# Query and key weights issued from ScalarE's DMA queue, token blocks left on SyncE's, and 14 more filler matmuls

## The chip, the cores and the metric

The kernel runs on one core of one Trainium2 chip. The metric is the device time of one execution in microseconds. Thirteen executions of the kernel before are at hand, and one more look at it with the hardware profiler on, which is itself one of the executions timed.

## The reference

A transformer block on 2048 tokens of 640 features, in bfloat16. With everything that is only shape taken out:

```python
h  = x + attn(layernorm(x), wq, wk, wv, wo, beta)     # x: [1, 2048, 640]
h2 = h + silu(layernorm(h) @ w1) @ w2                 # w1: [640, 1728]
# attn: 32 heads of 20, 4 segments of 512 tokens, one after the other
q, k, v = x @ wq, x @ wk, x @ wv                      # each weight [640, 640]
for s in range(4):
    p     = softmax(q_s @ k_s.T * 20**-0.5 + causal_mask)
    a_mem = (phi(q_s) @ M) / (phi(q_s) @ z + 1e-6)    # phi(t) = t+1 if t>0 else exp(t)
    o_s   = g * a_mem + (1 - g) * (p @ v_s)           # g = sigmoid(beta)
    M, z  = M + phi(k_s).T @ v_s, z + sum(phi(k_s))
out = concat(o) @ wo
```

## The kernel before

**Tiling.** Tokens come in blocks of 128, four blocks to a segment. Each of the four segments goes through the same stages: layer norm of its blocks (`n1_st`, `n1_rs`, `n1_ap` for statistics, reciprocal root and application), transposition into `xT`, projections `pr` to queries and keys (line 801) and `v` to values (line 773), scores `qk` (line 874), their exponentials `e` on ScalarE (line 885), causal masks on GpSimd (line 897), products with the values `av` (line 920), normalisation into `otok`, the output projection `wo` (line 1102), a second layer norm, and the two layers of the feed-forward part, `h1` (line 1126) and `h2` (line 1157). Stages of neighbouring segments are interleaved.

**Order.** Nothing is scheduled at run time. The table `ORDER` (line 355) lists every task by name, with the buffer slots that it takes and, behind a slash, the engine where there is a choice (`/A` ScalarE, `/D` VectorE). Each task, when its turn in the table comes, appends its instructions to the list of its engine; so the order on one engine is the order of the table cut down to that engine's tasks. `Tracker.add` (line 79) works out which semaphores each instruction has to wait for, and `Tracker.emit` (line 160) writes the lists, a wait in front of the instruction that needs it. Every transfer has a semaphore of its own.

**Transfers.** All go through the helper `dma` (line 535), which puts them on SyncE's list (`SP` in the code; `AC` is ScalarE). `load_x` (line 559) fetches token blocks, `load_w` (line 564) weights. The first nine transfers have no wait ahead of them: four token blocks (`x0`, `x2`, `x1`, `x3`, 160 KB each, in this order), then `w_q` (800 KB), `beta` (128 copies of 64 bytes), `w_k` (800 KB), `w_wv` (800 KB) and the next four blocks in one transfer (`x4`, 640 KB).

**The first 20 us.** TensorE begins with `fill54`: 54 matmuls of 256 columns on a tile of zeros (line 607), whose result nobody reads. Then come the transposes `n1_tp0` to `n1_tp3` (line 731), which read the normalised blocks. Their results are moved from PSUM to `xT` by `n1_te0`, `n1_te1` and `n1_te3` on ScalarE and `n1_te2` on VectorE (lines 740, 741). The raw query and key weights land in a part of the buffer `sT` and are rearranged head by head into `wqr` and `wkr` by `re_wq0` to `re_wq4` and `re_wk0` to `re_wk4`, some on VectorE (line 688), some on ScalarE (line 686). The first projections are `pr000` and `pr010`, which need the first two parts of `wqr`, then `pr001` and `pr011`, which need those of `wkr`; their results go to `QK` by `qe` tasks (lines 811, 812). GpSimd sets up constants and pads of the value tile meanwhile (`vpad1`, lines 614 to 616).

The place of the weights in the table, before the change, is this (first lines of `ORDER`; `w_q` and `w_k` are tasks of SyncE, so their place counts only against SyncE's other tasks):

```python
zpad:0 iota sel epsc x0:0 vpad0 mt2 x2:1 n1_st0:0 x1:2 x3:3 w_q:0 n1_st2:2 mta2 halfc mt0 mt1 n1_rs0 n1_st1:1
n1_st3:3 epsg0 n1_ap0:0 n1_rs2 fill54:0 n1_tp0:0 n1_te0/A:0 n1_rs1 n1_rs3 n1_ap1:1 n1_ap2:2 n1_tp1:2 n1_te1/A
n1_ap3:0 re_wq0/D:0 n1_tp2:4 n1_te2/D n1_tp3:6 n1_te3/A beta pr000:4 w_k zf0 re_wq1/A pr010:6 lsc0 re_wk0/D:0
```

A filler `fillN:S` writes N times into PSUM slot S; it waits until what was in that slot has been read. There are two besides `fill54`: `fill2` and `fill4`, near 160 us.

Of the kernel before, what the change touches and what calls it, by code (L numbers as in the profile page):

```python
# [324 lines left out]
D = 640  # L325
# [32 lines left out]
n1_ap3:0 re_wq0/D:0 n1_tp2:4 n1_te2/D n1_tp3:6 n1_te3/A beta pr000:4 w_k zf0 re_wq1/A pr010:6 lsc0 re_wk0/D:0  # L358
re_wk2/A pr001:5 re_wk1/D lsc1 mta1 lsc2 re_wk3/A qe000/D:0 pr011:7 w_wv:0 x4:4,5,6,7 qe001/A qe011/A:0 ex011:0 lsc3
re_wq4/D re_wq2/D pr020:5 qk0x0:0 e0x2:0 e0x0 qe010/D pr031:7 pr021:6 qk1x0:0 vpad1 mtb1 mm5 mm1 mk0x n1_st5:3  # L360
qe020/D:0 ph011:0 qe021/D n1_rs5 v00:4 n1_st6:1 n1_ap5:0 re_wk4/D qe031/A:0 re_wq3/A ex001:1 n1_st4:3 n1_st7:2
e1x2:1 e1x0 v01:6 mk1x pr030:0 ve00/A:0 ex021:0 ve01/A qk2x0:4 qe030/A av1x:1 ex031:2 av0x:2 e2x2:0 pr041:3 pr040:0
oe1x/A:0 e2x0 mt3 n1_rs4 qk3x0:4 e3x0:1 e3x2 n1_rs7 mta3 mtb3 mm11 mk2x n1_rs6 vt06:0 oe0x/D:1 ph001:1 vt09 kt01:0
vt03 tn0x:1 qe041/D:0 kt00:1 ex041:1 v03:2 qe040/D ph031:0 qk0yb0:4 nm0x:0,0 v02:0 e0yb2:0 ve03/D ph021:1 e0yb0
qk0ya0:4 tn1x:2 ve02/D nm1x:0 e0ya2:0 e0ya0 mk0yb mk3x av2x:3 oe2x/D:0 qk4x0:0 av0y:4 e4x2:0 e4x0 n1_ap6:2 av3x:6
mz00:5 tn2x:7 oe0y/D:1 oe3x/D:0 zf1 n1_ap7:1 nm2x:0 qk1yb0:0 vt00 vt010 vt08 vt01 ma00/A:0 e1yb2:0 e1yb0 n1_ap4:3
vt05 n1_tr5:0 mk4x v11:4 ve11/A:1 mk1yb mtb2 mm10 vt07 n1_tr6 vt04 vt011 vt02 mz01:7 qk1ya0:0 tn0y:6 nm0y:0 ma01/D:1
v12:4 ve12/D av4x:7 e1ya2:0 e1ya0 n1_tr4 n1_tr7 oe4x/A:1 tn3x:6 qk5x0:0 e5x0:0 e5x2 mm3 mk5x tn4x:7 nm3x:0 v10:4
qk6x0:0 kt03:0 nm4x:1 e6x0:1 kt02:1 v13:6 e6x2 ve10/D av5x:4 oe5x/D:1 ve13/A qk7x0:0 pr100:5 qe100/D:0 ph041:1
e7x0:0 mz02:4 e7x2 ma02/A:2 mk6x av6x:6 qk2yb0:0 mta0 mk7x e2yb2:1 e2yb0 mk2yb mtb0 tn5x:5 pr101:4 w_w2_1:0 w_w1_0:0  # L370
w_wo:0 oe6x/D:1 av7x:6 nm5x:1 av1y:7 w_w1_3 oe7x/D:0 qk2ya0:0 ex100:1 tn6x:6 qe101/D e2ya2:0 e2ya0 nm6x:1 ex101:0
pr130:5 tn7x:6 pr110:4 nm7x:1 qk3ya0:0 pr111:6 qe110/A:0 ph100:0 ph101:0 pr121:4 oe1y/D:0 ot0:0 qe111/D e3ya2:1
e3ya0 qk3yb0:0 e3yb0:0 wo0:6 qe130/D:0 e3yb2 qe121/D:0 ex110:0 rs0 w_w1_1 ot1 mm0 mzc0 av2y:4 oe2y/A:1 n2_st0:3
qk4ya0:0 mm9 mzc1 mk3yb mm6 mzc6 n2_rs0 mm2 wo1:6 rs1 n2_st1:1 w_w2_0 w_w1_4 n2_ap0:1 e4ya2:0 e4ya0 mz03:4 w_w1_2
qk4yb0:0 kt10:1 e4yb2:1 e4yb0 av3y:5 tn2y:6 pr141:7 n2_rs1 n2_tr0:0 mzc2 mzc3 mb00:0 mk4yb ma03/D:3 nm2y:1 n2_ap1:3
n2_tr1 ex111:1 qk5ya0:0 pr140:4 oe3y/A:1 qe141/A:0 tn3y:7 e5ya0:1 nm3y:1 e5ya2 pr120:6 mz10:7 tn1y:5 qk5yb0:0
qe120/A qe140/D av4y:4 ma10 nm1y:1 oe4y/D:0 ph110:0 e5yb2:0 h1_0_8_0:5 e5yb0 h1_0_1_0:7 th0_8_0:0 ex140:2 th0_1_0:1
tn4y:4 qk6ya0:0 pr131:6 e6ya2:0 e6ya0 s0_1_0:0 nm4y:1 s0_8_0 ph111:0 h1_0_0_0:7 th0_0_0:0 w_w2_2 s0_0_0 qe131/D
mk5yb h1_0_13_0:4 th0_13_0:1 qk6yb0:0 h1_0_10_0:5 h1_0_11_0:7 av5y:6 s0_13_0 e6yb0:1 e6yb2 w_w2_4 x8:8,9,10,11
kt11:1 w_w2_3 qk7ya0:0 h1_0_9_0:4 th0_10_0:1 th0_11_0:0 s0_10_0 e7ya0:1 s0_11_0 h1_0_7_0:5 th0_9_0:0 th0_7_0:1  # L380
oe5y/D:0 epsg1 e7ya2 tn5y:6 nm5y:1 s0_9_0 h1_0_2_0:7 h1_0_5_0:6 th0_2_0:0 s0_7_0 mk6yb mm4 th0_5_0:1 qk7yb0:0
e7yb2:0 ph140:0 s0_5_0 s0_2_0 h1_0_3_0:5 th0_3_0:1 h1_0_6_0:4 h1_0_4_0:6 av6y:7 e7yb0 s0_3_0 th0_4_0:1 s0_4_0
qk8a0:0 n1_st11:1 h1_0_12_0:5 th0_6_0:0 oe6y/A:0 s0_6_0 e8a0:0 mk7yb e8a2 h2_0_0:6 n1_st10:3 n1_rs10 mk8a av7y:4
th0_12_0:0 qk8b0:0 e8b0:0 ex120:2 e8b2 ex141:1 s0_12_0 n1_st8:2 n1_rs8 oe7y/D:1 n1_st9:0 n1_rs9 h2_0_1 h2_0_2 h2_0_3
qk8e0:0 e8e0:0 e8e2 ex130:0 n1_ap8:3 o0 h2_1_0:4 ph141:0 tn6y:6 tn7y:7 h2_1_1 vt16:0 mk8e ex131:1 mk8b qk9a0:0
e9a0:1 e9a2 nm7y:1 h2_1_2 h2_1_3 kt04:0 vt12 mz04:7 qk9b0:0 nm6y:0 n1_tr8:0 vt10 ph131:1 vt13 ot2 o1 mzc10 n1_ap9:3
mzc4 n1_rs11 av8:6 wo2:4 n1_ap11:1 ma04/A:4 ph120:0 rs2 e9b2:1 e9b0 oe8/A:1 qk10a0:0 vt18 tn8:6 ot3 out0 n1_tr9 vt19
nm8:0,0 n1_ap10:3 n1_tr11 e10a0:0 e10a2 wo3:4 qk10b0:0 n1_tr10 vt14 ex121:2 mk9b mb01:0 mk9a ad8:0 av9:6 e10b0:0
e10b2 rs3 oe9/D:1 kt14:0 vt110 n2_st3:3 mk10a mm7 qk10e0:4 e10e2:0 e10e0 mzc7 n2_rs3 mk10b mz11:0 ma11 tn9:2 pr200:1
nm9:0,0 n2_st2:1 n2_ap3:3 qk11a0:4 e11a0:1 e11a2 pr201:0 v20:2 mk10e mk11a mzc5 qk11b0:4 n2_rs2 mb02:0 mm8 mzc8  # L390
qe201/A:0 e11b0:1 ve20/D:0 e11b2 pr211:0 qe200/D av10:2 qk12a0:4 oe10/A:1 vt15 mzc9 mzc11 mb04:0 mk11b vt11 mb03:0
n2_ap2:1 qe211/D:0 e12a2:0 e12a0 ad9 tn10:2 nm10:0,1 ph130:0 kt13:1 out1 vt111 n2_tr2 n2_tr3 v21:0 ve21/A qk12b0:4
av11:2 vt17 oe11/D:1 ph121:1 mz14:0 e12b0:0 e12b2 ma14 h1_0_1_1:1 th0_1_1:0 h1_0_4_1:2 th0_4_1:1 qk13a0:4 e13a2:1
e13a0 kt12:0 h1_0_2_1:3 s0_1_1 s0_4_1 tn11:0 pr231:2 qk12e0:4 th0_2_1:1 nm11:0,0 mk13a mk12b mz13:0 mk12a s0_2_1
e12e2:0 e12e0 h1_0_6_1:3 qe231/D:0 h1_0_5_1:2 mz12:1 ma13 qk13b0:4 th0_5_1:1 th0_6_1:0 s0_5_1 s0_6_1 ma12 h1_0_8_1:0
mk12e h1_0_9_1:2 e13b0:1 e13b2 av12:1 qk14a0:4 pr210:3 th0_8_1:0 oe12/D:1 s0_8_1 v23:0 e14a2:0 th0_9_1:0 e14a0
qk14b0:4 e14b0:0 e14b2 s0_9_1 qe210/D ve23/D h1_0_7_1:3 h1_0_3_1:2 pr221:0 qk14e0:4 qe221/D:0 th0_3_1:0 th0_7_1:1
mk13b s0_3_1 mk14a e14e0:1 e14e2 s0_7_1 mk14b h1_0_10_1:1 av13:0 h1_0_0_1:3 qk15a0:4 ad11 mk14e ad10 oe13/D:0
th0_10_1:1 th0_0_1:0 s0_0_1 s0_10_1 pr241:0 tn12:2 av14:1 e15a2:1 e15a0 qk15b0:4 qe241/D:0 pr220:0 oe14/A:1
h1_0_13_1:1 e15b2:0 e15b0 nm12:0,1 mk15a th0_13_1:1 qe220/D mk15b ad12 s0_13_1 tn14:2 nm14:0,0 ex201:2 v22:4 ve22/A  # L400
ex220:0 tn13:0 av15:2 nm13:0,1 qk16a0:4 pr230:3 oe15/A:0 tn15:0 ph201:1 qe230/D e16a2:1 vt29:0 ad13 mb10:0 mb12:0
ad14 nm15:0,1 e16a0 h1_0_12_1:2 ex231:2 ad15 h1_0_11_1:3 th0_12_1:1 ex211:1 qk16b0:4 e16b0:0 e16b2 mk16b h2_2_0:0
h2_2_1 s0_12_1 th0_11_1:1 mk16a ph211:0 qk16e0:4 e16e2:1 s0_11_1 pr240:2 h2_2_2 ex200:1 ph200:0 h2_2_3 o2 e16e0
qe240/A ph220:0 ot5:0 qk17b0:4 wo5:2 ot6 ot4 vt26 e17b2:1 e17b0 rs5 mk16e mb13:0 av16:0 ph231:2 ex241:0 n2_st5:1
oe16/A:0 qk17a0:4 e17a2:1 wo4:2 e17a0 kt23:0 out2 ot7 rs4 n2_st4:3 ex210:2 kt20:1 vt211 ph210:0 h2_3_0:0 qk18b0:4
tn16:2 h2_3_1 h2_3_2 nm16:0,1 e18b0:0 e18b2 qk18e0:4 mk17b mb14:0 h2_3_3 n2_rs4 n2_rs5 wo7:2 n2_ap4:3 n2_tr4:0 mk18b
mk17a ex230:2 e18e2:0 e18e0 o3 qk18a0:4 n2_ap5:1 rs7 n2_st7:1 out3 mk18e ad16:0 vt22 vt20 e18a0:0 wo6:0 x12 vt21
n2_tr5 e18a2 av17:2 qk19b0:4 mk18a rs6 n2_st6:3 n2_rs7 e19b2:1 e19b0 oe17/A:0 mb11:0 n2_rs6 mz20:3 av18:0 mz23:1
ma20 n2_ap7:3 fill2:3 qk19a0:4 oe18/D:1 n2_tr7 e19a0:0 e19a2 mk19b mk19a n2_ap6:2 ma23 n2_tr6 vt210 vt24 tn18:2
nm18:0,1 vt25 vt28 vt27 vt23 fill4:0 tn17:0 qk20a0:4 e20a0:1 av19:2 e20a2 oe19/A:0 n1_st13:3 h1_1_0_0:3 th1_0_0:1  # L410
n1_st15:1 qk20b0:4 e20b0:1 nm17:0,0 ph241:1 s1_0_0:0 n1_st12:0 h1_1_1_0:2 e20b2 h1_1_3_0:0 th1_1_0:1 h1_1_7_0:3
th1_3_0:0 ex240:0 qk21b0:4 h1_1_2_0:1 e21b2:0 e21b0 ad18 n1_rs15 s1_1_0 n1_rs13 n1_rs12 n1_ap12:2 n1_ap15:3 mk20b
s1_3_0 n1_st14:1 th1_7_0:0 s1_7_0 h1_1_5_0:2 n1_rs14 th1_5_0:1 qk20e0:4 e20e2:0 h1_1_9_0:0 s1_5_0 n1_tr15:0 n1_tr12
n1_ap14:1 h1_1_10_0:3 th1_2_0:0 h1_1_4_0:2 th1_9_0:1 ex221:1 e20e0 s1_2_0 n1_tr14 s1_9_0 th1_10_0:1 s1_10_0 mk20a
mk21b mk20e th1_4_0:0 v30:0 qk21a0:4 n1_ap13:1 ve30/D:1 s1_4_0 ph230:0 e21a2:0 h1_1_6_0:3 v32:0 e21a0 qk22a0:4
av20:2 n1_tr13 kt21:0 mk21a ad17 th1_6_0:0 s1_6_0 av21:3 ve32/A tn19:0 oe20/D:1 nm19:0,0 pr311:2 e22a2:1 e22a0
# [33 lines left out]
def build(nc, es, A_x, A_wq, A_wk, A_wv, A_wo, A_beta, B_x, B_w1, B_w2, out):  # L450
    T = Tracker()
# [77 lines left out]
    def R(*items):  # L529
        r = []  # L530
        for a, subs in items:
            r += a.keys(subs)
        return r

    def dma(name, reads, writes, fn, prio, bw, kind="plain", lane=None, after=None):
        ln = T.lane(name) if lane is None else lane

        def emit(eng):
# [691 lines left out]
```

## Time and profile before

| | us |
|---|---|
| median of 13 executions | 320.0 (318.1 to 322.41) |
| the profiled execution | 321.41 |
| its span, first to last instruction | 319.7 |
| mean granted TensorE clock in it | 0.988 of full |

| engine | busy | share of the span |
|---|---|---|
| TensorE (PE) | 303.6 us | 95% |
| ScalarE (ACT) | 226.8 us | 71% |
| VectorE (DVE) | 220.2 us | 69% |
| GpSimd (POOL) | 144.9 us | 45% |

Names in the profile: PE is the matmuls, PEld the weight loads beside them, SPq the issue of transfers by SyncE. A row of the timeline gives start, duration, engine, line, operation, and in brackets how long the engine was idle before it and for whom. The chain that ended last is followed back from the last instruction, at each step to what released it; shares of the span are read from it. A wait that is not on this chain costs nothing while the chain stays as it is. The ends of matmuls are modelled, so a TensorE shown busy is not always at its peak. The granted clock is the share of full speed that the throttle let TensorE have. The time from the issue of a transfer to its landing is shown apart from the issue itself, which takes only the issuing engine's queue.

### The profile page before, as it was taken

What the parts mean: (1) busy time and instruction counts of PE and PEld (TensorE: products, weight loads), DVE (VectorE), ACT (ScalarE), POOL (GpSimd) and SP (SyncE); (2) the same over time, 40 slices, a digit from 0 to 9 for tenths busy, and PEclk for the clock granted to TensorE, in tenths of its full rate; (3) what the DMA queues carried; (4) which work ended last, traced back from release to release, by engine and by line L of the source; (5) the groups of instructions that cost most, each with busy time, mean ns of one, the idle gap of its engine ahead of it and who ended that gap; (6) DMA issues with size and microseconds to landing.
All of it is one profiled execution on the core that took longest, in us unless ns stands there. A gap on an engine that the chain in (4) does not pass through costs nothing.

```text
span 319.7 us, 7256 instructions
## 1 busy us (share of the span) xinstructions
PE 303.6 (95%) x2894; PEld 168.0 (53%) x2894; DVE 220.2 (69%) x488; ACT 226.8 (71%) x322; POOL 144.9 (45%) x282
## 2 busy tenths in 40 slices
PE   8799899999988999999969999999999999999996
PEld 6454454566554555555523444555664457654563
DVE  7588558877967865859887776469867666834703
ACT  1598798899988999899769896778769951004500
POOL 6336634433467665466854436344753731300000
PEclk9999799999999999999989999999999999999999
DMA  6813476958255320032582300040360004330002
GB/s 189 283 22 65 80 197 178 281 146 136 34 103 80 78 19 3 9 64 59 106 142 45 65 0 2 2 91 21 64 89 2 0 2 114 73 103 23 0 2 103
DMA packets 48353, 24.56 MB, mean 77 GB/s; under 512 B 38848, under 2 KB 47232, under 8 KB 48320
## 3 DMA queue, kind: packets, MB, share of 16 engines
q1 hardware_dynamic: 48320, 24.10, 34.3%
q8 instruction: 23, 0.38, 0.5%
q14 instruction: 10, 0.08, 0.1%
HBM read 10.33 MB, written 2.62 MB: 41 GB/s over the span
## 4 chain that ended last, share of the span: by engine, by line
PE 67%; DVE 11%; ACT 9%; DMA 7%; SPq 2%; issue 2%; POOL 1%; DVEq 0%; ACTq 0%
PE ps_all L1126 17%; PE ps_all L1157 16%; PE ps_all L801 10%; PE ps_all L874 6%; PE ps_all L1102 5%; PE ps_all L773 5%; PE ps_all L920 3%; ACT PTE L885 3%; DMA oT<-otok 3%; DMA sT<-in_A_wk_dram 3%; ACT PTB L885 2%; ACT PTA L885 2%; PE ps_all L949 2%; DMA hT<-xn_rot 1%; PE ps_all L953 1%
## 5 line engine op out<-in xcount | busy, mean ns | idle before, releaser
L1126 PE MATMUL ps_all<-hT,w_sb 128*128 128x512 bf16 (+3 forms) x350 | 68.9, 342 | 2.0 <-DMA hT<-xn_rot 1.5
L885 ACT ACTIVATE PTA<-ps_all 128x1024 bf16<-128x1024 f32 x64 | 62.4, 1026 | 9.2 <-PE ps_all L874 8.3
L1157 PE MATMUL ps_all<-w_sb,sT 128*128 128x320 bf16 x448 | 67.2, 300 | 0.4 <-DVE on L986 0.3
L885 ACT ACTIVATE PTB<-ps_all 128x1024 bf16<-128x1024 f32 (+1 forms) x64 | 58.9, 970 | 8.3 <-PE ps_all L874 8.2
L897 POOL TENSOR_SCALAR_AFFINE_SELECT PTB<-PTB 128x512 bf16<-128x512 bf16 x64 | 40.9, 639 | 43.5 <-ACT PTB L885 41.1
L1134 ACT ACTIVATE th<-ps_all 128x512 f32<-128x512 f32 (+2 forms) x70 | 34.6, 521 | 35.2 <-PE ps_all L1126 30.9
L1140 DVE SCALAR_TENSOR_TENSOR sT<-th,ps_all 128x512 bf16<-128x512 f32 (+2 forms) x70 | 38.8, 576 | 24.8 <-ACT th L1134 24.1
L1157 PEld LDWEIGHTS ps_all<-w_sb,sT 128*128 128x128 bf16 x448 | 40.7, 98 | 24.1 <-issue 7.2
L1126 PEld LDWEIGHTS ps_all<-hT,w_sb 128*128 128x128 bf16 (+1 forms) x350 | 31.8, 99 | 31.3 <-issue 7.7
L885 ACT ACTIVATE PTE<-ps_all 128x1024 bf16<-128x1024 f32 (+1 forms) x40 | 35.9, 944 | 5.2 <-PE ps_all L874 4.8
L897 POOL TENSOR_SCALAR_AFFINE_SELECT PTE<-PTE 128x512 bf16<-128x512 bf16 x40 | 25.7, 642 | 26.9 <-ACT PTE L885 25.5
L705 DVE BATCH_NORM_STATS2 stt<-x_tok 128x6 f32<-128x320 bf16 x64 | 27.9, 477 | 0.8 <-DMA x_tok<-in_A_x_dram 0.5
L1167 DVE SCALAR_TENSOR_TENSOR x_tok<-ps_all,x_tok 128x640 bf16<-128x640 f32 x16 | 13.0, 822 | 19.9 <-PE ps_all L1157 19.7
L1102 PE MATMUL ps_all<-wo_sb,oT 128*128 128x320 bf16 x160 | 24.1, 299 | 2.1 <-DMA oT<-otok 1.4
L773 PE MATMUL ps_all<-wv_sb,xT 128*128 128x320 bf16 x160 | 25.5, 309 | 0.1
L801 PE MATMUL ps_all<-xT,wqr 128*128 128x512 bf16 x100 | 24.6, 380 | 0.9 <-ACT xT L740 0.9
L801 PE MATMUL ps_all<-xT,wkr 128*128 128x512 bf16 x100 | 24.4, 380 | 0.7 <-DVE wkr L688 0.7
L994 POOL TENSOR_TENSOR otok<-on 128x320 bf16<-128x320 bf16 x24 | 19.1, 798 | 11.3 <-DVE on L986 11.3
L812 DVE CAST QK<-ps_all 128x512 bf16<-128x512 f32 x28 | 19.0, 685 | 7.4 <-PE ps_all L801 6.7
L874 PE MATMUL ps_all<-QK 20*128 20x256 bf16 (+3 forms) x360 | 20.8, 289 | 3.0 <-DVE oTs L935 1.8
L897 POOL TENSOR_SCALAR_AFFINE_SELECT PTA<-PTA 128x512 bf16<-128x512 bf16 x24 | 15.4, 643 | 12.7 <-ACT PTA L885 12.7
L935 DVE TENSOR_SCALAR oTs<-ps_all,lsc 128x512 bf16<-128x512 f32 (+1 forms) x25 | 15.6, 627 | 7.3 <-PE ps_all L920 7.1
(78 smaller groups left out, 406.8 us busy)
## 6 DMA issues: line engine op xcount, KB each, us to landing
out_dram<-x_tok SPq DMA_DIRECT2D x16, 160.0 KB, 1.9
w_sb<-in_B_w_dram SPq DMA_DIRECT2D x5, 432.0 KB, 6.3
x_tok<-in_A_x_dram SPq DMA_DIRECT2D x3, 640.0 KB, 6.1
w_sb<-in_B_w_dram SPq DMA_DIRECT2D x3, 640.0 KB, 5.0
QKV<-QK SPq DMA_DIRECT2D x16, 72.0 KB
sT<-in_A_wq_dram SPq DMA_DIRECT2D x1, 800.0 KB, 6.6
sT<-in_A_wk_dram SPq DMA_DIRECT2D x1, 800.0 KB, 9.2
wv_sb<-in_A_wv_dram SPq DMA_DIRECT2D x1, 800.0 KB, 10.9
```

The lines of the kernel that those rows point to most:

```text
L705: T.add(DV, lambda e, hh=hh: e.bn_stats(out=stt[:, s, 6 * hh:6 * hh + 6], in_=xb[:, 320 * hh:320 * hh + 320]), reads=R((xa, xsub)), writes ...
L773: fns.append(lambda e, c=c, hh=hh: e.matmul(bank(ps, hh)[:, 0:320], lhsT=xT[:, c, 128 * i:128 * i + 128], rhs=wv_sb[:, c, 320 * hh:320 * h ...
L801: fns = [lambda e, kc=kc: e.matmul(bank(ps), lhsT=wt[:, kc, c, :], rhs=xT[:, kc, :], start=(kc == 0), stop=(kc == NC - 1)) for kc in range ...
L874: fns.append(lambda e, j=j, o=o, r=r, q0=q0, q1=q1, qa=qa, ka=ka: e.matmul(ps_all[:, o:o + q1 - q0], lhsT=ka[32 * r:32 * r + DH, 128 * j:1 ...
L885: T.add(AC, lambda e: e.activation(out=pt[:, pta.slot, q0:q0 + 2, 0:width], in_=sc3[:, b0:b0 + 2, 0:width], func=ACT.Exp, scale=SCALE), re ...
L897: fns.append(lambda e, v=v: e.affine_select(out=v, in_=v, pattern=[[0, 4], [1, 128]], compare_op=ALU.is_ge, fill=0.0, base=0, channel_mult ...
L994: T.add(PO, lambda e: e.tensor_tensor(out=o_dst, in0=on[:, ona.slot, 0, :].rearrange("p (i x) -> p i x", i=4), in1=on[:, ona.slot, 1, :].r ...
L1102: fns.append(lambda e, c=c, hh=hh: e.matmul(bank(ps, hh)[:, 0:320], lhsT=oT[:, c, 128 * i:128 * i + 128], rhs=wo_sb[:, c, 320 * hh:320 * h ...
L1126: fns = [lambda e, c=c: e.matmul(bank(ps)[0:fw, lo:hi], lhsT=w1_sb[:, c, 128 * f:128 * f + fw], rhs=hT[:, c, lo:hi], start=(c == 0), stop= ...
L1134: T.add(AC, lambda e: e.activation(out=th[0:fw, tha.slot, lo:hi], in_=bank(ps)[0:fw, lo:hi], func=ACT.Tanh, scale=0.5), reads=R((ps, [0])) ...
L1140: T.add(DV, lambda e: e.scalar_tensor_tensor(out=sT[0:fw, f, lo:hi], in0=th[0:fw, tha.slot, lo:hi], scalar=1.0, in1=bank(ps)[0:fw, lo:hi], ...
L1157: fns.append(lambda e, f=f, fw=fw, hh=hh: e.matmul(bank(ps, hh)[:, 0:320], lhsT=sT[0:fw, f, 128 * i:128 * i + 128], rhs=w2_sb[0:fw, f, 320 ...
```

## The change

The helper takes the engine that issues the transfer, and `w_q` and `w_k` are given ScalarE. Their names keep their places in `ORDER`; since they are now tasks of ScalarE, those places count against ScalarE's other tasks. In ScalarE's list `w_q` becomes the first instruction, ahead of the load of the activation table, and `w_k` stands between `n1_te3` and `zf0`; neither has a wait of its own. SyncE's list loses the two and is otherwise the same: four token blocks, `beta`, `w_wv`, `x4`.

Four fillers are added to the table: `fill8` in slot 0 between `n1_tp3` and `pr000`, `fill1` in slot 2 before `qk0ya0` (31.5 us in the profile before), `fill4` in slot 7 before `qk10e0` (97.7 us), and `fill1` in slot 3 ahead of the tasks that follow at 160.8 us. The rest of the table is the same names in the same order, with other line breaks. Lines below the table move down by one.

```diff
 ORDER
-n1_ap3:0 re_wq0/D:0 n1_tp2:4 n1_te2/D n1_tp3:6 n1_te3/A beta pr000:4 w_k zf0 re_wq1/A pr010:6 lsc0 re_wk0/D:0
+n1_ap3:0 re_wq0/D:0 n1_tp2:4 n1_te2/D n1_tp3:6 n1_te3/A beta fill8:0 pr000:4 w_k zf0 re_wq1/A pr010:6 lsc0
...
+e0yb0 fill1:2 qk0ya0:4 tn1x:2 ve02/D nm1x:0 e0ya2:0 e0ya0 mk0yb mk3x av2x:3 oe2x/D:0 qk4x0:0 av0y:4 e4x2:0 e4x0
...
+e10b0:0 e10b2 rs3 oe9/D:1 kt14:0 vt110 n2_st3:3 mk10a mm7 fill4:7 qk10e0:4 e10e2:0 e10e0 mzc7 n2_rs3 mk10b mz11:0
...
+vt210 vt24 fill1:3 tn18:2 nm18:0,1 vt25 vt28 vt27 vt23 fill4:0 tn17:0 qk20a0:4 e20a0:1 av19:2 e20a2 oe19/A:0
...
-    def dma(name, reads, writes, fn, prio, bw, kind="plain", lane=None, after=None):
+    def dma(name, reads, writes, fn, prio, bw, kind="plain", lane=None, after=None, eng=SP):
         ln = T.lane(name) if lane is None else lane
 
-        def emit(eng):
+        def emit(_):
             extra = R(*after[1]()) if after else []
-            T.add(SP, lambda e: fn(e), reads=R(*reads) + extra, writes=R(*writes), lane=ln)
+            T.add(eng, lambda e: fn(e), reads=R(*reads) + extra, writes=R(*writes), lane=ln)
         cost = {"tr": 1.31, "plain": 0.47, "sb": 0.72, "bc": 2.9}[kind]
-        t = G.task(name, {SP: cost}, emit, reads, writes, prio, mode=kind, bw=bw)
+        t = G.task(name, {eng: cost}, emit, reads, writes, prio, mode=kind, bw=bw)
...
-    def load_w(k, dst, src, prio, bw, wr, after=()):
-        dma("w_" + k, [], wr, lambda e: e.dma_start(out=dst, in_=src), prio, bw, after=after)
+    def load_w(k, dst, src, prio, bw, wr, after=(), eng=SP):
+        dma("w_" + k, [], wr, lambda e: e.dma_start(out=dst, in_=src), prio, bw, after=after, eng=eng)
...
-    load_w("q", wraw[:, 0, :, :], cw(A_wq), -96, 2.5, [(sT0, ["q"])])
-    load_w("k", wraw[:, 1, :, :], cw(A_wk), -95, 2.5, [(sT0, ["k"])])
+    load_w("q", wraw[:, 0, :, :], cw(A_wq), -96, 2.5, [(sT0, ["q"])], eng=AC)
+    load_w("k", wraw[:, 1, :, :], cw(A_wk), -95, 2.5, [(sT0, ["k"])], eng=AC)
```

## The prediction

> **What bounds the kernel now.** I read the page first: TensorE is busy for 95% of the span, and two thirds of the chain that ended last are TensorE.
>
> ```profile
> PE 303.6 (95%) x2894; PEld 168.0 (53%) x2894; DVE 220.2 (69%) x488; ACT 226.8 (71%) x322; POOL 144.9 (45%) x282
> ...
> PE 67%; DVE 11%; ACT 9%; DMA 7%; SPq 2%; issue 2%; POOL 1%; DVEq 0%; ACTq 0%
> ```
>
> So a delay anywhere on TensorE is a delay of the end, unless a later gap gives it back. The change moves two transfers of the first 15 us, so the second view is the chain of waits there.
>
> ```profile
> 3.72 9.25 DMA sT<-in_A_wk_dram
> 12.98 1.37 DVE wkr L688 x2
> 14.36 0.05 issue
> 14.40 3.41 PE ps_all L801 x15
> ```
>
> Here is the bound of the stage: the key weights (`w_k`) are issued at 3.72 and land at 12.97; VectorE rearranges the first part (`re_wk0`), and only then, at 14.40, does the first key projection (`pr001`) start. From 14.40 on the work runs engine to engine without waiting for a transfer. What moves the landing of `w_k` moves the kernel. The query weights (`w_q`) are not on this chain: issued at 2.67, 6.6 us to landing, so there at 9.3, and `re_wq0` at 9.88 waited for nothing.
>
> The third view is the timeline, of SyncE's queue (its row for `beta` left out) and then of ScalarE:
>
> ```profile
> 0.80 1.83 SPq L562 DMA_DIRECT2D x_tok<-in_A_x_dram  x4
> 2.67 0.43 SPq L565 DMA_DIRECT2D sT<-in_A_wq_dram  x1
> ...
> 3.72 0.43 SPq L565 DMA_DIRECT2D sT<-in_A_wk_dram  x1
> 4.19 0.53 SPq L565 DMA_DIRECT2D wv_sb<-in_A_wv_dram  x1
> 4.76 1.20 SPq L562 DMA_DIRECT2D x_tok<-in_A_x_dram  x1
> ```
>
> ```profile
> 9.41 1.90 ACT L740 ACTIVATE xT<-ps_all 128x640 bf16<-128x640 f32 x3 [7.33 <-PE ps_all L731]
> ...
> 12.98 1.65 ACT L686 ACTIVATE wkr<-sT 128x400 bf16<-128x400 bf16 x5 [0.73 <-DMA sT<-in_A_wk_dram]
> ```
>
> SyncE waits for nothing and has issued everything by 6 us. ScalarE sits for 7.33 us until the first transposes of the tokens come from TensorE, then empties three of them (`n1_te0`, `n1_te1`, `n1_te3`, starting at 9.41, 10.01 and 10.60).
>
> The fourth is the table by stretches, in thirds of 10.2 us:
>
> ```profile
> 32.68:36.09 3.41, 2.30 (x48) 1.45 (x49) 2.28 (x7) 3.18 (x6) 2.08 (x4) 0.95 0.55 107
> 36.09:39.50 3.41, 3.41 (x23) 1.83 (x22) 1.13 (x4) 1.91 (x3) 2.79 (x6) 0.55 0.35 67
> 39.50:42.90 3.40, 3.28 (x39) 2.04 (x40) 2.50 (x8) 3.17 (x5) 0.00 (x0) 1.00 0.57 122
> ```
>
> First pair after the stretch: its length and TensorE's busy time; the column before the last two is the granted clock. A stretch in which TensorE was busy for 2.30 of 3.41 us is followed by one at about half clock (0.55). In that one, ten `L773` matmuls stand on the chain for 2.75 us; ten later ones for 1.36. Half a stretch of idleness thus costs about 1.4 us more afterwards.
>
> [...] This trace has one issuer, so it shows no sharing; it shows the issue time, 0.43 us each. [...] it records the standalone semaphore waits[...]. In 15 places on ScalarE and VectorE such a wait was already met while the instruction ahead of it still waited; in none did it run before that instruction's wait was met, by up to 4.7 us (on VectorE met at 252.34, run at 257.06, 0.04 after the wait ahead was met). I go by the trace. [...] a 128x400 `wkr` copy took 1.23 us beside GpSimd's memsets (12.78 to 14.05), the same form on `wqr` 0.27.
>
> **The change, part by part.**
>
> *`w_q` to ScalarE.* It leaves at 0.80 instead of 2.67, ahead of the table load, which starts some 0.43 later; ScalarE is idle until 9.41, so that costs nothing. It now shares the engines with the four token blocks. The blocks are 655 KB; [...] block four is complete only when about 1.3 MB have moved. At 300 GB/s from 1.75 us (first packet) that is near 6.4, plus 0.5 to land: 6.9, where its statistics started at 6.11. So they come up to 0.8 late (bounds 0 and 1.2). The cover is `fill54`: it holds TensorE until 9.09 while the first normalised block was ready near 7.5, and the third at 8.2. Cost 0, at most 0.3 if the cover is used up. Earlier arrival gains nothing, as `re_wq0` stands behind `n1_ap3`, which waited for TensorE.
>
> *`w_k` to ScalarE.* Its place in the order is after `n1_te3`, so on ScalarE it stands behind three instructions that wait for TensorE. By the behaviour above it leaves when `n1_te3`'s wait is met, about 10.6: **6.9 us later than now**. Behind it on ScalarE are `zf0` and `re_wq1`; the issue (0.43, nearest row; up to 1.2 as for the last issue on SyncE) runs beside the 0.7 us eviction, so they lose 0 to 0.5, and what `re_wq1` feeds (`pr010`) ends near 13.8 either way.
>
> Landing: first packet 0.95 after issue (0.80 to 1.75 for the first block), so 11.55; 40 packets on each engine at 55 ns are 2.2 us; 0.45 to land: 14.2 alone, the lower bound. But `w_v` and the next token block (1.47 MB) are still moving. They now stand in front: before, all had landed at 16.77 with 0.82 MB of `w_k` among them; without it, and with the thin stretches (105 GB/s at 7 to 8 us) partly filled, they end near 12.5 on most engines. [...] one engine is 1.5 us behind in the trace (its last piece of `w_k` came at 12.97, the others' by 11.48), so up to 16.4. Everything together cannot take longer than before: 16.8, the upper bound. I take 15.6: 2.65 late.
>
> Given back: at 15.6 GpSimd is through with its memsets and copies (14.82 before), so the first `wkr` copy takes 0.27 and not 1.23. The step from landing to `pr001` shrinks from 1.43 to about 0.5. TensorE restarts at 16.1, not 14.40: **+1.7 us (0.3 to 2.9)**. All that follows (`qe000`, `re_wk2`, the first scores) hangs on `pr001` or on queues behind `re_wk0` and `re_wk2`, so the delay is carried on.
>
> *Clock.* TensorE ends `pr010` near 13.8 and is then idle to 16.1, 2.3 us. A 3.41 us stretch with all of that is busy for 1.1, well under 2.30[...]. So a half-clock stretch is likely (three in four), over the 15 matmuls of `L801` that take 3.41 us at full clock: **+1.4 us**, the cost of the stretch at 36 us (0 to 1.7).
>
> *Fillers.* 8, 1, 4 and 1, at about 0.108 us each when warm (halved clock: 0.21). `fill8` takes 0.86 in the 0.88 gap before `pr000`; the four take 0.43 in the 0.86 gap at 97.7; single ones 0.11 in gaps of 0.34 (31.5) and 0.27 (160.8). They wait only for evictions already done. Cost 0; if a gap is gone, at most their 1.5 together. They might spare a half-clock stretch, but the two in mid-span (36.1, 165.8) follow gaps of 0.9 and 1.5 that one matmul does not fill: 0.
>
> *`beta`, `w_v` and the next tokens* leave SyncE up to 1 us earlier; nobody waited for them.
>
> **Sum.** 1.7 + 1.4 = 3.1 us against the profiled execution's 321.4 us (span 319.7 and 1.7 around it), 0.4% above the median of the runs, 320.0. Put on the median: **323.0**.
>
> **Rivals.**
> - *Late, but without the half clock.* +1.7: 321.7. [...]
> - *No late issue: the sequencer passes the waiting evictions.* Then `w_k` leaves near 2 us behind `w_q`. [...] it is complete when 3.3 MB have moved instead of 2.3, about 12 to 13 plus up to 2, one us late, mostly given back by the copy: 320.5, no change. Against it: the 15 waits.
> - *Faster.* The same early issue, and two rows fill the thin stretches (241 and 198 GB/s at 3 to 5 us, 105 and 213 at 7 to 9, against 380 later, some 0.76 MB or 2 us of transfer lost). `w_k` then lands by 11.5, its copies run before the memsets, and `pr001` follows `pr010` at 13.7: -0.7, and with one half-clock stretch spared -2.1: 318. It decides for faster if `w_k` is issued before about 4 us and lands before 12. Against it: the place in the order.
> - *The fillers as a cost:* +0.5 to 1.5 where gaps have closed; inside the range.
>
> **How the numbers follow.** Half of one per cent (1.6 us) is about what a measurement of this kernel can tell from no change. Late with half clock 0.60 (323.0, own range 321.6 to 325.0), late without 0.20 (321.7, half of it under 321.6), early and shared 0.13 (320.5), early and faster 0.07 (318). Slower: 0.60 nearly whole, 0.10, little else: 0.72. Same: 0.10, most of 0.13 and edges: 0.21. Faster: 0.07. Range 319.5 to 325.4: it leaves out the faster case and the worst sum (2.9 + 1.7 + fillers).
>
> **What would show it.** The issue of `w_k` on ScalarE's queue at 10.6, a landing at 15 to 16.5, `re_wk0` with a 0.3 us first copy, TensorE idle for some 2.3 us before the first `wkr` matmul at about 16.1, a clock near 0.5 in the 3.4 us behind it. An issue of `w_k` before 4 us would make the prediction wrong in its main step; a start of `pr001` at 16 with an unchanged time would mean that a later gap takes the delay up.

## The result: 323.4 us, slower by 1.3%

| | before | after |
|---|---|---|
| median | 319.42 us (48 runs, 316.21 to 323.28) | 323.43 us (11 runs, 321.33 to 326.81) |
| ratio of the times | | 1.0134, interval 1.0101 to 1.0168 |
| profiled execution, and its span | 321.41, 319.7 | 324.0, 322.3 |
| mean granted clock in it | 0.988 | 0.995 |
| first projection to keys (`pr001`) starts at | 14.40 | 17.07 |

The ratio is taken over the fast executions alone, those at most 1.5% above the fastest of their kernel, so it is not the quotient of the two medians.

The page of the kernel after, engines and the shares of the chain that ended last:

```profile
PE 304.7 (95%) x2908; PEld 169.2 (52%) x2908; DVE 219.8 (68%) x488; ACT 226.9 (70%) x322; POOL 144.7 (45%) x282
...
PE 66%; DVE 11%; ACT 9%; DMA 8%; SPq 2%; issue 2%; POOL 1%; DVEq 0%; ACTq 0%
```

TensorE has only the 14 fillers more to do and still bounds the kernel; from profile to profile its busy time rose by 1.1 us and the span by 2.6; the rest of these 2.6 us is waiting. The chain of waits of the kernel after, from the token block that it waited for to the key projections (start, duration, what):

```profile
1.27 5.29 DMA x_tok<-in_A_x_dram
...
10.07 0.47 PE ps_all L732 x5
10.53 0.02 issue
10.56 1.30 ACT xT L741 x2
11.87 4.70 DMA sT<-in_A_wk_dram
16.57 0.02 issue
16.59 0.43 DVE wkr L689 x2
17.02 0.04 issue
17.07 3.41 PE ps_all L802 x15
```

Before, the transfer of `w_k` stood on this chain from 3.72. Now it begins at 11.87, because ScalarE gets to it only then, and the chain reaches further back: through the evictions `n1_te0` and `n1_te1`, the transposes and the statistics to a token block that took 5.29 us. The timeline of the kernel after shows both halves of that (the brackets are the engine's idle time and whom it waited for):

```profile
0.81 0.46 ACTq L566 DMA_DIRECT2D sT<-in_A_wq_dram  x1
...
6.58 0.89 DVE L706 BATCH_NORM_STATS2 stt<-x_tok 128x6 f32<-128x320 bf16 x2 [1.55 <-DMA x_tok<-in_A_x_dram]
...
11.87 0.38 ACTq L566 DMA_DIRECT2D sT<-in_A_wk_dram  x1
...
17.07 2.33 PE L802 MATMUL ps_all<-xT,wkr 128*128 128x512 bf16 x10 [2.11 <-DVE wkr L689]
```

The second statistics start at 6.58; before they started at 4.12, and VectorE did not wait for them:

```profile
4.12 0.83 DVE L705 BATCH_NORM_STATS2 stt<-x_tok 128x6 f32<-128x320 bf16 x2
```

Where the tokens stand is seen in the DMA queues of the stretch from 3 to 5 us (packets, MB, and the time of the packets as a share of the 16 engines' time, which can overlap), first after, then before; q10 carries ScalarE's transfers, q1 SyncE's:

```profile
q10 hardware_dynamic: 567, 0.72, 97.3%
q1 hardware_dynamic: 57, 0.05, 7.8%
```

```profile
q1 hardware_dynamic: 388, 0.44, 78.2%
```

In these 2 us `w_q` has the engines nearly to itself (0.72 MB against 0.05), though three token blocks were issued on the other queue at 1.27 to 2.2. The tokens had lost time before that, too: from 2 to 3 us all queues together moved 91 GB/s, where before it was 289. The second block landed at 6.56 instead of 3.50, the fourth at 7.87 instead of 5.28.

Paired instruction by instruction, the trace after is 2.66 us later than the one before from 17 us on, and 2.6 us later at the end. That the two agree is partly chance: in between the difference moves where one of the two has a half-clock stretch (before at 36.1 and 165.8, after at 37.4) or a late transfer.

### The profile page after: what moved, and what is told of

Read it like the earlier page. It is cut to its first block, busy times and chain, and to the rows that moved or that the text cites. A ratio compares the mean times of both kernels' runs of the same rounds, so it can differ in the third digit from the quotient of the medians.

```text
span 322.3 us, 7284 instructions
## 1 busy us (share of the span) xinstructions
PE 304.7 (95%) x2908; PEld 169.2 (52%) x2908; DVE 219.8 (68%) x488; ACT 226.9 (70%) x322; POOL 144.7 (45%) x282
## 3 DMA queue, kind: packets, MB, share of 16 engines
HBM read 10.33 MB, written 2.62 MB: 40 GB/s over the span
## 4 chain that ended last, share of the span: by engine, by line
PE 66%; DVE 11%; ACT 9%; DMA 8%; SPq 2%; issue 2%; POOL 1%; DVEq 0%; ACTq 0%
PE ps_all L1127 17%; PE ps_all L1158 16%; PE ps_all L802 10%; PE ps_all L875 6%; PE ps_all L774 5%; PE ps_all L1103 5%; PE ps_all L921 4%; DMA oT<-otok 4%; ACT PTE L886 3%; ACT PTB L886 2%; ACT PTA L886 2%; DVE stt L706 2%; PE ps_all L950 2%; DMA x_tok<-in_A_x_dram 2%; DMA sT<-in_A_wk_dram 1%
## 5 line engine op out<-in xcount | busy, mean ns | idle before, releaser
L1127 PE MATMUL ps_all<-hT,w_sb 128*128 128x512 bf16 (+3 forms) x350 | 67.7, 337 | 2.4 <-DMA hT<-xn_rot 1.9
L1135 ACT ACTIVATE th<-ps_all 128x512 f32<-128x512 f32 (+2 forms) x70 | 34.5, 522 | 35.7 <-PE ps_all L1127 31.5
```

Of the source, the lines that this page charges most:

```text
L1127: fns = [lambda e, c=c: e.matmul(bank(ps)[0:fw, lo:hi], lhsT=w1_sb[:, c, 128 * f:128 * f + fw], rhs=hT[:, c, lo:hi], start=(c == 0), stop= ...
L1135: T.add(AC, lambda e: e.activation(out=th[0:fw, tha.slot, lo:hi], in_=bank(ps)[0:fw, lo:hi], func=ACT.Tanh, scale=0.5), reads=R((ps, [0])) ...
```

## The experiments

The results of all of them are in this table. "Start" is that of `pr001` in the one profiled execution, "exponentials" the first of ScalarE; ratios are to the kernel before, run beside it on the same chip, with their intervals. For `w_k` alone and for the gap filled there are only six executions each.

| kernel | w_k issued, landed | start | exponentials | median | ratio |
|---|---|---|---|---|---|
| before, three profiled executions | 3.72; 12.97, 12.41, 11.65 | 14.40, 14.19, 13.70 | 18.15, 17.93, 17.43 | 319.0 to 319.9 | 1 |
| after | 11.87, 16.57 | 17.07 | 20.81 | 323.43 | 1.0134 (1.0101 to 1.0168) |
| `w_q` alone on ScalarE | 3.30, 11.80 | 14.97 | 18.70 | 320.32 | 1.0040 (1.0014 to 1.0066) |
| `w_k` alone on ScalarE | 10.33, 16.40 | 16.90 | 20.64 | 322.75 | 1.0100 (1.0039 to 1.0161) |
| fillers alone | 3.72, 12.38 | 13.74 | 17.47 | 320.11 | 1.0005 (0.9979 to 1.0031) |
| after, `w_k` early | 1.30, 11.62 | 15.25 | 18.97 | 321.53 | 1.0075 (1.0049 to 1.0101) |
| after, gap filled | 12.06, 16.85 | 17.34 | 21.08 | 323.02 | 1.0148 (1.0091 to 1.0206) |
| `w_q` in five pieces | 3.15, 11.79 | 14.01 | 17.74 | 319.51 | 1.0032 (1.0005 to 1.0059) |
| before, `beta` behind `w_k` | 3.15, 11.20 | 13.56 | 17.81 | 319.31 | 1.0023 (0.9989 to 1.0058) |
| tokens on both queues | 2.21, 10.98 | 13.08 | 17.33 | 320.52 | 1.0050 (1.0024 to 1.0075) |
| the same, two edits more | 2.23, 11.11 | 13.11 | 16.84 | 317.74 | 0.9975 (0.9948 to 1.0003) |
| the same without `fill8` | 2.21, 11.20 | 12.96 | 16.69 | 320.91 | 1.0022 (0.9993 to 1.0052) |

### `w_q` alone, `w_k` alone, the fillers alone

The theory was that the late issue of `w_k` is the cost. The rival was that the tokens, made late by `w_q`, cost it alone. Each part of the change was done by itself.

```diff
-    load_w("k", ..., [(sT0, ["k"])], eng=AC)
+    load_w("k", ..., [(sT0, ["k"])])            # w_q alone; no fillers
```

> Only the query weights go to ScalarE's queue; the key weights stay on SyncE behind beta, and the four added fillers are out. Theory A (the cost is the late issue of the key weights behind the waiting evictions, made later still by the tokens that the query weights overtake): the tokens are late as in the changed kernel (second statistics near 6.6 us), but w_k leaves SyncE near 3.2 and lands by about 13, so the first key projection starts near 15.0 instead of 14.4: +0.6 us, 0.2%. Theory B (the overtaken tokens alone are the cost): +2.7 us as in the changed kernel. Theory C (fillers): 0.

```diff
-    load_w("q", ..., [(sT0, ["q"])], eng=AC)
+    load_w("q", ..., [(sT0, ["q"])])            # w_k alone; no fillers
```

> Only the key weights go to ScalarE's queue, behind the third eviction; the query weights stay on SyncE, no added fillers. Theory A: tokens on time, the eviction's wait met near 10.55, w_k issued at 10.6, landed 4.7 us later at 15.3, first key projection at 15.8: +1.4 us, 0.45%. Theory B: 0. If the sequencer could pass the waiting evictions, the issue would stand near 1.3 us and the projection at 14.4 or before.

```diff
 load_w as before; ORDER of the kernel after      # fillers alone
```

> The four added fillers alone (8, 1, 4 and 1 matmuls), both weights on SyncE as before. Theory A: all lie in gaps; fill8 (0.86 us) fills the gap of 0.88 before the first query projection; no change, within 0.3 us, the start of the first key projection at 14.4. Theory C (the fillers cost time): up to +1.5 us. If they spare half-clock stretches: up to -1.4 us with a higher granted clock.

`w_q` alone cost 0.4%: `w_k`, left on SyncE, landed at 11.80 and `pr001` started at 14.97. It had to wait for `pr010`, which the tokens had made late (statistics at 6.76 and 8.80 for the second and fourth block). `w_k` alone cost 1.0%. Its timeline has tokens in time and the late issue all the same:

```profile
10.33 0.43 ACTq L563 DMA_DIRECT2D sT<-in_A_wk_dram  x1
10.41 0.71 ACT L738 ACTIVATE xT<-ps_all 128x640 bf16<-128x640 f32 x1
...
16.42 0.74 DVE L686 COPY wkr<-sT 128x400 bf16<-128x400 bf16 x4 [5.46 <-DMA sT<-in_A_wk_dram]
...
16.90 1.47 PE L799 MATMUL ps_all<-xT,wkr 128*128 128x512 bf16 x6 [3.39 <-DVE wkr L686]
```

The issue lies within 0.1 us of the start of `n1_te3` (10.41), as in the kernel after (both 11.87). A landing 4.7 us after the issue had been expected, at 15.3; it took 6.1 us. With `w_q` on SyncE's queue the transfers ahead were later than in the kernel after: `w_q` landed at 9.79 instead of 6.11, `w_v` and `x4` at 12.59 and 14.30 instead of 11.38 and 13.01. So the late issue by itself brings the start of `pr001` to 16.90, nearly the 17.07 of the kernel after, and is most of the cost (1.0100, the interval is wide); the tokens are the smaller part. The two don't add up: with `w_q` gone early, `w_k` landed 4.70 after its issue, and that gave back most of what the tokens had cost. The fillers alone measured nothing.

### `w_k` early, still on ScalarE

```diff
 ORDER
-zpad:0 iota sel epsc x0:0 vpad0 mt2 x2:1 n1_st0:0 x1:2 x3:3 w_q:0 n1_st2:2 ...
+zpad:0 iota sel epsc x0:0 vpad0 mt2 x2:1 n1_st0:0 x1:2 x3:3 w_q:0 w_k n1_st2:2 ...
```

> The changed kernel with w_k moved in the table right behind w_q, so that both are the first instructions of ScalarE's queue (0.8 and 1.25 us); fillers kept. If the late issue were all of the cost: the first key projection follows the query projections at 13.7, -0.7 us against before. If a transfer on ScalarE's queue overtakes the tokens whole, as w_q did in the changed kernel: the tokens come some 2.2 us later still (second statistics near 8.8), the first key projection near 17.2, about +2.8 us, as slow as the changed kernel although w_k has been there for long.

The place in the table and not the queue is what makes `w_k` late: put ahead of the evictions, it left at 1.30 and landed at 11.62. It did not hold the tokens up as far as expected; the second statistics came at 6.74, as with `w_q` alone, and only the last block was later (9.02). The start, 15.25, is again that of a `pr010` made late by tokens. 0.75% are left, so with `w_k` early the change still loses. That is 2.4 us, of which the start, 1.1 us later than the mean of before, is less than half; where the rest goes isn't shown.

### Is a large transfer taken whole?

```diff
-    load_w("q", wraw[:, 0, :, :], cw(A_wq), ..., eng=AC)
+    five transfers for w_q, c = 0 to 4:  out=wraw[:, 0, c, :], in_=A_wq[128 * c:128 * c + 128, :]
```

> w_q alone on ScalarE's queue, w_k on SyncE as before, no added fillers, and w_q cut into five transfers of 160 KB (the size of a token block), issued one after the other from 0.8 us on. Theory 'the engines take a whole large transfer of one queue before they turn to the other': the tokens now come between the pieces, third block by 5.6, fourth by 6.8 (7.2 and 7.6 with w_q in one piece), second statistics at 4.3 to 5.0 instead of 6.76, n1_te3 at 10.6 to 11.0 instead of 12.05, pr001 at 14.3 to 14.6, ratio 1.001. Theory 'ScalarE's queue goes first as long as it holds anything': tokens as late as in one piece (fourth block 7.6 or later), pr001 at 15.0, ratio 1.004.

The statistics of the four blocks in the timeline of the kernel with five pieces:

```profile
3.67 0.89 DVE L710 BATCH_NORM_STATS2 stt<-x_tok 128x6 f32<-128x320 bf16 x2 [1.09 <-DMA x_tok<-in_A_x_dram]
...
4.72 0.83 DVE L710 BATCH_NORM_STATS2 stt<-x_tok 128x6 f32<-128x320 bf16 x2
6.45 0.89 DVE L710 BATCH_NORM_STATS2 stt<-x_tok 128x6 f32<-128x320 bf16 x2 [0.66 <-DMA x_tok<-in_A_x_dram]
7.79 0.89 DVE L710 BATCH_NORM_STATS2 stt<-x_tok 128x6 f32<-128x320 bf16 x2 [0.20 <-DMA x_tok<-in_A_x_dram]
```

With the same bytes on the same queue, the second block now came by 4.4 instead of 6.7, and `pr001` started at 14.01 instead of 14.97. From 3 to 5 us each of the two queues moved 0.33 MB: the pieces and the blocks took turns, and a queue that always goes first is ruled out by that. The engines did not fall idle from 2 to 3 us either (250 GB/s; with `w_q` in one piece 37). The later two blocks fit only in part: 6.4 and 7.8 against 5.6 and 6.8 expected, and the fourth came no sooner than with `w_q` in one piece (7.6). The ratio, 1.0032, can't be told from that of `w_q` in one piece (1.0040), though the start is 1 us sooner in the profile.

That a large transfer is always taken whole is not so, however. In the kernel with `w_k` early, the 800 KB of `w_k` stood behind those of `w_q` on ScalarE's queue, with tokens waiting on SyncE's. These are the queues from 5.5 to 7.5 us there, when `w_q` had landed (6.34):

```profile
q10 hardware_dynamic: 321, 0.41, 59.0%
q1 hardware_dynamic: 286, 0.33, 48.4%
```

So the first large transfer had the engines to itself (97.3% of their time, in the kernel after), and the second, of the same size, shared them (59.0% and 48.4%). Why the first went through in one and the second did not stays open.

### Is the idle TensorE behind the wait a cost of its own?

```diff
 ORDER
-re_wk0/D:0 re_wk2/A pr001:5 re_wk1/D ...
+re_wk0/D:0 re_wk2/A fill20:5 pr001:5 re_wk1/D ...
```

> The kernel after with 20 more fillers (256 columns, some 2.2 us when warm) directly ahead of pr001, in its slot 5: TensorE works through the gap in which it waited for wkr. Issue of w_k (11.9), its landing (16.6) and the start of pr001 (17.1) stay as in the kernel after. Theory 'idle TensorE behind the wait costs clock': fewer half-clock stretches, about 1.4 us less than after, near 322.0. Theory 'the wait alone is the cost': time as after, 323.4, ratio about 1.012; a filler that runs past the landing would add up to 0.5.

The time did not fall, so filling the gap buys nothing that could be measured; the 1.4 us in question are 0.4%, though, and the interval of six executions is 0.6% to each side. The table by stretches says more. It has length, TensorE's busy time, and further right the granted clock, then DMA share and GB/s. The kernel after:

```profile
13.50:16.90 3.40, 1.46 (x7) 0.49 (x5) 0.31 (x2) 0.33 (x2) 2.41 (x8) 1.00 0.66 233
16.90:20.30 3.40, 3.23 (x15) 1.38 (x15) 3.37 (x15) 2.76 (x8) 0.00 (x0) 1.00 0.00 0
...
34.00:37.40 3.40, 2.17 (x54) 1.04 (x52) 2.18 (x6) 2.87 (x5) 2.49 (x4) 1.00 0.39 72
37.40:40.80 3.40, 3.40 (x25) 1.98 (x24) 2.45 (x7) 2.47 (x4) 1.71 (x3) 0.50 0.35 68
```

And with the gap filled:

```profile
34.60:38.00 3.40, 1.65 (x50) 0.88 (x48) 2.77 (x7) 2.35 (x3) 2.52 (x4) 0.99 0.39 72
38.00:41.40 3.40, 3.34 (x29) 1.90 (x22) 2.33 (x7) 2.84 (x5) 1.55 (x3) 0.50 0.33 63
```

In the kernel after, 2.11 us of waiting lie in a stretch with 1.46 us of work, and the next is at full clock. The half clock comes at 37.4, behind a stretch with more work (2.17 us), in many small matmuls. It comes there with the gap filled too. So in these two executions the wait for `w_k` cost its length and no clock. Nor does the form of the matmuls settle it: in the second profile of before the like stretch, 32.35 to 35.76, had 2.18 us of the same small matmuls, and the clock behind it was full (granted clock 1.000 over that execution).

### Was the first profile of before an ordinary one?

> The kernel before, unchanged, looked at once more. In its first profile w_k landed at 12.97 and pr001 started at 14.40; the kernel with only the added fillers, whose transfers are the same, had 12.38 and 13.74. If the first profile was an ordinary execution: pr001 at 14.2 to 14.5 again, and the change's delay is 2.7 us. If its w_k was late by chance: landing at 12.3 to 12.6, pr001 at 13.7 to 13.9, and the delay against an ordinary execution is 3.2 to 3.4, which would account for more of the measured 4.3.

> A third look at the kernel before, for the same question: pr001 at 14.2 to 14.5 if the first profile was ordinary, at 13.7 to 13.9 if its w_k was late by chance; both values would mean that the start of pr001 differs by 0.7 us from execution to execution.

Nothing was changed here. The starts were 14.19 and 13.70; of the third profile, the two lines that answer to the chain shown in the prediction:

```profile
11.67 0.74 DVE L688 COPY wkr<-sT 128x400 bf16<-128x400 bf16 x4 [0.48 <-DMA sT<-in_A_wk_dram]
...
13.70 2.32 PE L801 MATMUL ps_all<-xT,wkr 128*128 128x512 bf16 x10
```

Here `w_k` landed at 11.65 and its copies were through before `pr010` had ended; `pr001` has no wait in brackets at all. The landing differs by 1.3 us from execution to execution, the start of `pr001` by 0.7, since `pr010` is a floor. The first profile was the latest of the three, and the only one with half-clock stretches in mid-span (granted clock 0.988, in the others 1.000). Against their mean, 14.1, the change delays `pr001` by 3.0 us and not by 2.7.

### Towards a better version

If the landing of `w_k` is late in some executions, it should help to let it go sooner without touching the tokens. First, `beta` with its 128 packets of 64 bytes was moved behind it:

```diff
 ORDER (SyncE)    ... x3 w_q w_k beta w_wv x4
 ORDER (others)   zf0, lsc0, lsc1 moved behind re_wk3; lsc2 ahead of lsc3
```

> The kernel before with beta issued behind w_k on SyncE's queue instead of ahead of it, and beta's first readers (zf0, lsc0, lsc1, lsc2) moved behind the re_wk tasks. If the 128 small packets of beta thin the transfers at 7 to 8 us, w_k lands near 12.0 instead of 12.4 to 13.0, its copies are done before pr010 ends (13.7), and pr001 starts at 13.7: -0.7 us against the profile before, 318.7, ratio 0.998. If beta is not what holds it, w_k lands 0.1 to 0.5 earlier only (issue 0.57 earlier) and pr001 starts at 14.0 to 14.4: ratio 1.000.

`w_k` landed at 11.20 and `pr001` started at its floor, 13.56, and still the time is that of before. The exponentials came at 17.81, that is 4.25 behind `pr001` and not 3.74 as before: the moved readers of `beta` had cost elsewhere what the transfer gave (TensorE waited 0.36 us for `wqr`; with two of the readers moved on, below, it is 3.73 again). Then the tokens were put on both queues and the weights behind them on SyncE:

```diff
-        load_x(b, 1, -100 + b, ...)
+        load_x(b, 1, -100 + b, ..., eng=(SP, AC, SP, AC)[b])
 ORDER (beta and its readers as above)
-... n1_rs2 fill54:0 n1_tp0:0 ...
+... n1_rs2 fill44:0 n1_tp0:0 ...
```

> Candidate for a better version: the two queues used for the token blocks (x0, x2 on SyncE, x1, x3 on ScalarE, all issued by 1.3 us), w_q and w_k behind them on SyncE (issued near 1.8 and 2.2, not 2.67 and 3.72), then beta, w_v, x4; readers of beta moved as in the run with beta behind w_k; fill54 cut to fill44, since the tokens come sooner. If the issue time of w_k sets the start of pr001: w_k lands at 11.3, pr010 ends at 12.6, pr001 at 12.6 to 13.0 against 14.4: -1.5 us, 317.9, ratio 0.995. If bandwidth sets it, w_k lands at 12 to 12.5, pr001 at 13.0: -0.7 to -1.0 from fewer fillers alone, ratio 0.997. Rival: TensorE idles at 8 to 9 us for want of tokens and loses clock, ratio 1.000 or above.

`pr001` started at 13.08, 0.6 to 1.3 us sooner than in the three profiles of before, and the time rose by 0.5%. In the 22 executions the mean granted clock was 0.992; it was 0.995 in those of before beside them. Two more edits:

```diff
-... n1_te3/A pr000:4 ...            ... lsc2 lsc3 re_wq4/D re_wq2/D pr020:5 ...
+... n1_te3/A fill8:0 pr000:4 ...    ... re_wq4/D re_wq2/D lsc2 lsc3 pr020:5 ...
```

> The run with the tokens on both queues, mended where its profile showed the gain of pr001 (13.08) going: lsc2 and lsc3 moved behind re_wq2 on VectorE, so that pr020 does not wait for wqr (0.37 us), and fill8 put ahead of pr000 into the 1.1 us in which TensorE waited. First scores at 16.4 instead of 16.94 (17.08 in the run with fillers only), first exponential at 16.8. If only the start of the chain counts: -0.65 us against the run with fillers only, 319.0, ratio 0.998. If the earlier start goes with more half-clock stretches, as the mean granted clock of that run's executions (0.992 against 0.995 of before) suggests: 320, ratio 1.003.

The first scores now come at 16.44, and the median is the lowest of all, 317.74. From the timeline:

```profile
0.80 0.88 ACTq L561 DMA_DIRECT2D x_tok<-in_A_x_dram  x2
...
2.23 0.53 SPq L564 DMA_DIRECT2D sT<-in_A_wk_dram  x1
...
13.11 2.32 PE L800 MATMUL ps_all<-xT,wkr 128*128 128x512 bf16 x10
...
16.44 0.34 PE L873 MATMUL ps_all<-QK 20*128 20x256 bf16 x8
```

Taken over the two ratios to before, it beats the kernel after by 1.6% (1.0134 / 0.9975); over the kernel before the gain is 0.25%, and its interval still touches 1. Which of the two edits did it:

```diff
-... n1_te3/A fill8:0 pr000:4 ...
+... n1_te3/A pr000:4 ...
```

> The best kernel so far (tokens on both queues, lsc2 and lsc3 behind re_wq2, ratio 0.9975) without its fill8 ahead of pr000; TensorE waits there for 1.1 us. First scores stay at 16.4 and the first exponential at 16.8. If fill8 is what raised the mean granted clock of the executions from 0.992 (tokens on both queues, without these two edits) to 0.996, it falls to about 0.992 and the time rises by about 1 us, ratio 1.001. If fill8 does nothing, as the four fillers added to the kernel before did nothing: 317.7, ratio 0.9975.

Without `fill8` the start of the chain stays (exponentials at 16.69) and the gain is gone: 1.0022, mean granted clock 0.992 against 0.996. So in this version eight fillers in a gap of about 1 us seem to be worth some 0.5%, while the fillers added to the kernel before were worth nothing. It is not certain: the two ratios come from different chips, each with its own executions of before, and their intervals meet (up to 1.0003, from 0.9993). The half clock that was met in the profile without `fill8` came at 165.0, far behind the filler; how a filler at 10 us bears on it is not settled.

## Why the prediction was right in its number, and where not in its steps

The predicted 323.0 stands beside 323.43, and the sign and the main mechanism held. The terms did not all have their size, and that the sum came out so near is luck.

- **`w_k` leaves with `n1_te3`'s wait: right.** The sequencer did not pass the waiting evictions in any of the three kernels that had the transfer there: issue 11.87, 10.33 and 12.06, with `n1_te3` starting at 11.87, 10.41 and 12.05. The rivals with an early issue fall with it. Forced by hand, the early issue also loses (1.0075), so the faster rival, the two queues together filling the thin stretches, would not have come true with it either: its gate, an issue before 4 us and a landing before 12, was met (1.30 and 11.62), and the tokens were what it had left out.
- **"Cost 0, at most 0.3" for `w_q`: the step that failed.** It took the tokens and `w_q` to share the engines evenly, so that with the 655 KB of blocks as many of `w_q` would have moved, 1.3 MB. That was the author's estimate; the trace of before, with one issuer, shows no sharing. Here, from 3 to 5 us, `w_q` took 97.3% of the engines' time and the tokens queued on SyncE's queue 7.8%, while with `w_k` early the next 800 KB on ScalarE's queue shared them with the tokens (59.0% and 48.4%). The statistics of the second block were 2.46 us late and those of the fourth 2.51 (8.62 against 6.11), not 0.8, the cover of `fill54` was used up, and `n1_te3` started at 11.87 instead of 10.60. By itself this costs 0.4%. (The sum in that step was off as well: 1.3 MB at 300 GB/s from 1.75 are done at 6.1, not 6.4.)
- **+1.7 for the start of `pr001`: the term that was mis-sized.** It measured +2.67, inside its bounds of 0.3 to 2.9, and +3.0, just outside, against the mean of the three profiles of before. The issue was 1.3 us later than worked out, for the tokens' sake; landing from issue took 4.70 where 5.0 was taken. The 5.0 was the author's estimate, with `w_k` sharing the engines with `w_v` and `x4` on their way; that was not shown: those two had landed by 13.01, and from 13.0 to 16.6 ScalarE's queue moved 0.81 MB and SyncE's nothing. The first `wkr` copies went as said: 0.43 for the two that `pr001` needs, where they had taken 1.37: GpSimd's memsets, which had run beside them from 12.78 to 14.07, ran from 14.05 to 15.34 now, before the copies at 16.59.
- **+1.4 for a half clock behind the wait: wrong.** The stretch behind the gap, 16.90 to 20.30, had the full clock (1.00). The three-in-four chance was the author's estimate, read off one pair of stretches, by busy time alone; 1.46 us of 128x512 matmuls held the clock, 2.17 us of small ones lost it, and 2.18 us of small ones held it in another execution.
- **Fillers at nothing: right** (1.0005).
- **The sum: near by luck.** 3.0 for the start of `pr001` is less than the 4.3 that the ratio gives (3.2 to 5.4 from its interval). The number came out because the delay was taken too small and a clock term was added that was not where it was put.

What makes up the rest of the 4.3 is known in part only. Some may be clock: the executions of the kernel after had a mean granted clock of 0.993, those of before 0.995; over all executions of the study 0.005 of clock goes with 1.4 us, so that this would be some 0.5. It is not all of it: among executions with a granted clock of 0.998 or more, the kernel after took 321.8 on average (5 of them) and before 318.2 (67), 3.6 us less. Some is later transfers. `w_k` alone, profiled, had the full clock from start to end, as the second profile of before had; it is 2.7 us behind that at `pr001` and 5.2 at the end (321.1 against 315.9). 1.5 of the added 2.5 us come near 272, where TensorE waits for a transfer of attention outputs that it doesn't wait for in that profile of before. The kernel after has the same wait (first `w_k` alone, then after):

```profile
274.23 1.53 PE L1100 MATMUL ps_all<-wo_sb,oT 128*128 128x320 bf16 x10 [1.51 <-DMA oT<-otok]
```

```profile
273.22 1.53 PE L1103 MATMUL ps_all<-wo_sb,oT 128*128 128x320 bf16 x10 [0.99 <-DMA oT<-otok]
```

These are single traces, and why a later start should make this transfer late is not shown.

## What to carry to other kernels

A transfer given to a busy engine's queue is an instruction of that engine: work out when the engine reaches its place in the order, and which evictions it waits behind, before asking what the second queue may bring (here 11.87 behind the evictions, 1.30 ahead of them). A large transfer on a second queue can hold up small urgent ones on the first (here `w_q` had 97.3% of the engines' time, and the second token block landed at 6.56 instead of 3.50). With the small ones first on both queues and the large ones behind them, `pr001` started 0.6 to 1.3 us sooner here, though no sure gain in time came of it. Profile several executions before pricing a landing, since what is to be gained by an earlier transfer ends at the next floor, here the end of `pr010`, right behind which `pr001` started at 13.70 in the third profile of before.

## What was not expected of the hardware

- From 3 to 5 us the DMA engines moved 389 GB/s with `w_q` on ScalarE's queue and tokens waiting on SyncE's, and 220 GB/s before with everything on SyncE's. From 2 to 3 us it was the other way: 91 against 289. The transfer of `w_q` took 5.3 us from issue to landing instead of 6.6.
- The first 800 KB on ScalarE's queue kept the tokens on SyncE's waiting (97.3% of the engines' time); the 800 KB behind it, with `w_k` early, shared the engines with them (59.0% and 48.4%).
- The landing of the same transfer in the unchanged kernel, issued at 3.72 each time, was 12.97, 12.41 and 11.65.
- Whether TensorE keeps its clock did not follow its busy time: 1.46 of 3.40 us kept it, 2.17 lost it, 2.18 kept it in another execution.
- A start earlier by 0.6 us or more need not show in the time: 1.0022 at a mean granted clock of 0.992, and 0.9975 at 0.996 with eight matmuls more that compute nothing.
